# Linear attention and a feed-forward layer in one kernel: projection on half the array's rows, VectorE in written order, an early x chunk

## The chip, the cores and the metric

The kernel runs on one core of a Trainium2 chip. The metric is the device time of that core in microseconds (us). The engines are TensorE (PE in the profile, with its weight loads as PEld), VectorE (DVE), ScalarE (ACT), GpSimd (POOL), and SyncE (SP), whose queue issues nearly all DMAs.

## The reference, cut to what matters

```python
batch, n_heads, seq, head_dim = (8, 8, 576, 64);  d_feat = 128     # q, k, v, w_phi
n_tokens, d_model, d_ff = (4608, 512, 2048)                        # w_in, w_out, alpha

def phi(x):
    proj = np.einsum('bhsd,df->bhsf', x, w_phi)
    proj = proj - np.max(np.abs(proj), axis=-1, keepdims=True)
    return np.concatenate([np.exp(proj), np.exp(-proj)], axis=-1)
q_p, k_p = (phi(q), phi(k))
kv = np.einsum('bhsf,bhsd->bhfd', k_p, v)
z = np.sum(k_p, axis=2)
num = np.einsum('bhsf,bhfd->bhsd', q_p, kv)
den = np.einsum('bhsf,bhf->bhs', q_p, z)[..., None] + 1e-06
attn = num / den

x = attn.transpose(0, 2, 1, 3).reshape(B * S, H * D)
h = x @ w_in
g = np.maximum(h, 0.0) + alpha * np.minimum(h, 0.0)
out = g @ w_out
```

All data are float32; the weights of the feed-forward layer come as float64 and are decoded on the chip.

## The kernel before, in words

**Attention.** The 64 (batch, head) products go two heads at a time: 32 pairs. A pair's k and q lie transposed in one tile `raw`, head 0 on partitions 0 to 63 and head 1 on 64 to 127, in nine tiles of 128 columns (tile 4 holds the last 64 keys and the last 64 queries). `project` (line 202) multiplies each tile with `w_sb`, a block-diagonal 128 x 256 matrix that holds `w_phi` twice: one matmul over all 128 array rows gives both heads' projections. It does so in five chunks (`CHUNKS`) of 2, 2, 1, 2 and 2 tiles into `pj`, two PSUM buffers. Of each chunk VectorE takes the absolute maximum `m` (L221) and writes `t = pj - m` to SBUF (L222); then the buffer is free. For keys ScalarE makes `exp(t)` and `exp(-t)` (`k_exp`, tiles `xk` and `k4`). `k_acc` (L255) forms kv on TensorE, each head on its own 64 array columns. `k_sum` (L245 to L247) adds the key tiles on VectorE in three steps (`y`, `z`, `z`), and `k_z` (L265) sums the rest over partitions by a matmul with ones. `kv_turn` (L276) transposes; `q_exp` (L286, L292) transposes the query part of `t`, and ScalarE takes exponentials; `num` (L302) and `den` (L316) are the two products, the latter on 32 array columns each. The denominator then goes through a small DMA into 9 columns (`d9`), is inverted on VectorE (L332, L333), written to `rec_d` in device memory and read back over all partitions as `rr`; GpSimd multiplies (L343), and SP stores the result to `x_d`.

**Feed-forward layer.** All products are made of three passes with a high and a low part, so a matrix product of one 128 x 128 block takes three matmuls of 512 columns. Its 2048 hidden columns are split: pass 1 does the first five blocks of 128 (`NF1`), pass 2 the other eleven. Tokens go in nine chunks of 512 (`C2`). Pass 1 of chunks 0 to 6 runs between the attention's work: `fetch` (L388) reads the chunk from `x_d` as `xr`, `split` makes `xh` on VectorE (L95) and `xl` on GpSimd (L98), `up` gives `h` (L372 to L374), `act_g` (L161 to L168) forms `g`, `gh` and `gl` on ScalarE and VectorE, and `down` gives `o` (L378 to L380), stored to `part_d`. Behind the attention come the first step of pass 2 with chunk 0 (`load_x(0)`: four reads of 256 KB, L497, and the casts to `x2hl`), pass 1 of chunks 7 and 8, and then the rest of pass 2. `decode` (L129) makes float32 weights of float64 ones: a scale on ScalarE (L138), four integer steps on VectorE (L139 to L142), the rest on GpSimd and ScalarE; ten blocks (`NA`) are written to `w_d` and read back later by POOL's queue (L463).

**Order.** Every unit of work stands in a list `todo` with a time in units of one pair: pair i's unit comes at i plus its entry in `AT`, and chunk c of pass 1 between its start and that of the next chunk, which `F0`, `FR` and `FB` give. The list is sorted, and in that order TensorE and SP get their instructions (`manual_schedule`, L456). A planner with its own model of durations sets the order on VectorE, ScalarE and GpSimd; it held to the written order where `keep_in_program_order` stands. Each engine then works through its list strictly in order.

## Time and profile before

| what | value |
|---|---|
| median of 3 runs | 1289.01 us (1287.61 to 1291.89) |
| the profiled execution | 1286.31 us, its span 1284.5 us |
| mean granted TensorE clock | 0.978 |
| PE busy | 1201.5 us (94%) |
| DVE busy | 661.7 us (52%) |
| ACT busy | 553.7 us (43%) |
| POOL busy | 205.1 us (16%) |

The first 135 us are attention and decoding alone (pairs 0 to 8), up to about 657 us attention and pass 1 alternate, and the rest is the feed-forward layer alone. In the rows of groups, a name such as `pj<-w_sb,raw` is output and inputs, `128*128 128x256` the array part and the output, and the part behind the bar the busy time, the mean time of one, and the idle time ahead of them with what ended it. A float32 matmul leaves two records (576 for the 288 projections), a matmul of the feed-forward layer and a transpose one. In a timeline, records of one kind in a row are merged into one line with their count, and the second column is the time from the first one's start to the last one's end.

### The profile page before, as it was taken

What the parts mean: (1) busy time and instruction counts of PE and PEld (TensorE: products, weight loads), DVE (VectorE), ACT (ScalarE), POOL (GpSimd) and SP (SyncE); (2) the same over time, 40 slices, a digit from 0 to 9 for tenths busy, and PEclk for the clock granted to TensorE, in tenths of its full rate; (3) what the DMA queues carried; (4) which work ended last, traced back from release to release, by engine and by line L of the source; (5) the groups of instructions that cost most, each with busy time, mean ns of one, the idle gap of its engine ahead of it and who ended that gap; (6) DMA issues with size and microseconds to landing.
All of it is one profiled execution on the core that took longest, in us unless ns stands there. A gap on an engine that the chain in (4) does not pass through costs nothing.

```text
span 1284.5 us, 16532 instructions
## 1 busy us (share of the span) xinstructions
PE 1201.5 (94%) x6272; PEld 909.1 (71%) x6272; DVE 661.7 (52%) x1134; ACT 553.7 (43%) x1113; POOL 205.1 (16%) x209
## 2 busy tenths in 40 slices
PE   6888699989999899998959999999999999999998
PEld 4555467667766577665647888888888888888886
DVE  6678766656665665667715275333333242324232
ACT  4556455535555454454623364333333233333332
POOL 2223412121130301315404043000000000000000
PEclk9999899999999899999979999999999999999999
DMA  4244425243433524435254141211202020202010
GB/s 160 82 128 140 131 91 159 91 158 100 159 99 117 175 77 147 128 111 180 80 199 148 41 140 58 75 57 42 98 1 99 1 99 1 98 1 99 1 66 33
DMA packets 67806, 124.18 MB, mean 97 GB/s; under 512 B 14224, under 2 KB 19472, under 8 KB 67088
## 3 DMA queue, kind: packets, MB, share of 16 engines
q1 hardware_dynamic: 67008, 117.90, 28.3%
q0 software_dynamic: 720, 5.24, 1.1%
q8 instruction: 49, 0.80, 0.3%
q14 instruction: 29, 0.24, 0.1%
HBM read 89.27 MB, written 33.70 MB: 96 GB/s over the span
## 4 chain that ended last, share of the span: by engine, by line
PE 67%; DVE 13%; DMA 12%; ACT 3%; issue 3%; POOL 2%; SPq 1%; DVEq 0%; ACTq 0%; POOLq 0%
PE h L372 9%; PE h L374 9%; PE h L373 9%; PE po L378 7%; PE po L379 7%; PE po L380 7%; PE pj L213 5%; PE kv L255 3%; DMA xr<-x_d 3%; DMA rr<-rec_d 2%; DVE t L222 2%; DMA raww<-w_out_dram 2%; DVE m L221 2%; DMA raww<-w_in_dram 2%; DMA rec_d<-r 2%
## 5 line engine op out<-in xcount | busy, mean ns | idle before, releaser
L163 DVE SCALAR_TENSOR_TENSOR g<-r,aln,g 128x512 f32<-128x512 f32 x144 | 112.4, 781 | 289.3 <-ACT g L162 287.5
L161 ACT ACTIVATE r<-h 128x512 f32<-128x512 f32 x144 | 86.0, 597 | 271.4 <-PE h L374 271.3
L213 PE MATMUL pj<-w_sb,raw 128*128 128x256 f32 x576 | 158.8, 400 | 43.8 <-DVE t L222 37.1
L213 PEld LDWEIGHTS pj<-w_sb,raw 128*128 128x128 f32 x576 | 109.1, 196 | 74.8 <-issue 46.2
L378 PE MATMUL po<-gh,w 128*128 128x512 f32 x396 | 155.2, 392 | 0.0
L379 PE MATMUL po<-gh,w 128*128 128x512 f32 x396 | 155.1, 392 | 0.0
L380 PE MATMUL po<-gl,w 128*128 128x512 f32 x396 | 153.2, 392 | 0.0
L98 DVE TENSOR_TENSOR gl<-g,gh 128x512 fp32r<-128x512 f32 x144 | 105.4, 732 | 74.1 <-ACT gh L94 73.5
L94 ACT CAST gh<-g 128x512 fp32r<-128x512 f32 x144 | 89.6, 622 | 101.5 <-DVE g L163 101.1
L221 DVE TENSOR_REDUCE m<-pj 128x4 f32<-128x512 f32 (+1 forms) x160 | 100.3, 628 | 23.1 <-PE pj L213 22.4
L222 DVE TENSOR_TENSOR t<-pj,m 128x512 f32<-128x512 f32 (+1 forms) x160 | 100.8, 631 | 2.1
L372 PE MATMUL h<-xh,w 128*128 128x512 f32 x180 | 88.1, 489 | 13.2 <-DVE xh L95 13.2
L372 PE MATMUL h<-x2hl,w 128*128 128x512 f32 x220 | 87.0, 396 | 13.9 <-ACT x2hl L94 13.9
L343 POOL TENSOR_TENSOR s<-s,rr 128x576 f32<-128x576 f32 x31 | 44.5, 1434 | 281.7 <-DMA rr<-rec_d 272.1
L378 PE MATMUL o<-gh,w 128*128 128x512 f32 x180 | 85.4, 475 | 2.6 <-ACT gh L94 1.6
L373 PE MATMUL h<-x2hl,w 128*128 128x512 f32 x220 | 86.6, 394 | 0.0
L374 PE MATMUL h<-x2hl,w 128*128 128x512 f32 x220 | 86.6, 394 | 0.0
L380 PEld LDWEIGHTS po<-gl,w 128*128 128x128 f32 x396 | 74.3, 188 | 16.7
L379 PEld LDWEIGHTS po<-gh,w 128*128 128x128 f32 x396 | 74.3, 188 | 16.7
L378 PEld LDWEIGHTS po<-gh,w 128*128 128x128 f32 x396 | 74.3, 188 | 16.7
L162 ACT ACTIVATE g<-h 128x512 f32<-128x512 f32 x144 | 85.6, 595 | 0.0
L294 ACT ACTIVATE qf<-qt 128x512 f32<-128x512 f32 x128 | 68.8, 599 | 30.5 <-PE qt L292 30.3
(77 smaller groups left out, 2084.6 us busy)
## 6 DMA issues: line engine op xcount, KB each, us to landing
raw<-kq_dram SPq DMA_DIRECT2D x32, 576.0 KB
xr<-x_d SPq DMA_DIRECT2D x17, 1024.0 KB
v<-v_dram SPq DMA_DIRECT2D x32, 320.0 KB
rr<-rec_d SPq DMA_DIRECT2D x64, 144.0 KB
x_d<-s SPq DMA_DIRECT2D x32, 288.0 KB
part_d<-os SPq DMA_DIRECT2D x36, 256.0 KB
pt<-part_d SPq DMA_DIRECT2D x9, 1024.0 KB
raww<-w_in_dram SPq DMA_DIRECT2D x32, 256.0 KB
```

The lines of the kernel that those rows point to most:

```text
L94: return act.copy(dst, src)
L98: return eng.tensor_tensor(dst, src, f(hi), op=ALU.subtract)
L163: dve.scalar_tensor_tensor(g, r, aln[:, ff : ff + 1], g, op0=ALU.mult, op1=ALU.add)
L213: pe.matmul(ps[:, j].rearrange("p h f -> p (h f)"), lhsT=c["raw"][:, tp * P : (tp + 1) * P], rhs=w_sb, start=True, stop=True,)
L221: dve.tensor_reduce(m, ps, axis=AX.X, op=ALU.max, apply_absolute_value=True)
L222: dve.tensor_tensor(c["t", ch][:, :, j0 : j0 + w].rearrange("p h j f -> p j h f"), ps, m.unsqueeze(3).broadcast_to([P, w, 2, FD]), op=ALU. ...
L372: pe.matmul(ps, lhsT=wt[0][:, ws], rhs=xh, start=n == 0, stop=False)
L373: pe.matmul(ps, lhsT=wt[1][:, ws], rhs=xh, start=False, stop=False)
L374: pe.matmul(ps, lhsT=wt[0][:, ws], rhs=xl, start=False, stop=n == NK - 1)
L378: pe.matmul(ps, lhsT=wt[2][:, ws], rhs=gh, start=first, stop=False)
L379: pe.matmul(ps, lhsT=wt[3][:, ws], rhs=gh, start=False, stop=False)
L380: pe.matmul(ps, lhsT=wt[2][:, ws], rhs=gl, start=False, stop=last)
```

## The change

It has five parts.

1. **Projection.** `w_sb` is now `w_phi` once on partitions 0 to 63 and once on 64 to 127. Each head has its own matmul with 64 array rows and 128 output columns, into a `pj` buffer of its own, so one chunk takes both buffers. There are three chunks of 4, 3 and 2 tiles instead of five.
2. **z.** For the first nine pairs (`ZP`) `k_sum` does nothing, and `k_z` has ten matmuls (five key tiles, two heads) instead of two.
3. **VectorE's order** is now the written one too. So that each VectorE step can have a time of its own, `decode`, `act_g`, `split`, `k_sum` and the denominator's steps are cut into units with offsets (`WE`, `WO`, `FG`, `FX`, `FS`, `ks`, `d9`, `rr`, `xs`), and the times in `AT` are new.
4. **Chunk 0 of pass 2** is read and cast inside `todo` (`first_x`, at `X0T`), by one read of 1024 KB, and no more behind the attention.
5. Pass 1's chunks start 0.2 to 0.3 pairs later (`F0`, `FB`), the fetch of a chunk stands 0.6 instead of 0.5 pairs ahead of it. The last pair's multiply with `rr` goes from VectorE to GpSimd.

```diff
-CHUNKS = ((0, 1), (2, 3), (4,), (5, 6), (7, 8))
+CHUNKS = ((0, 1, 2, 3), (4, 5, 6), (7, 8))
+ZP = 9
 AT = dict(
     ld=-0.95,
-    p=(0.0, 0.10, 0.36, 0.46, 0.60),
-    ke=(0.30, 0.48),
-    ks=0.50,
-    ka=0.90,
-    kz=1.150,
-    kt=1.153,
-    kr=1.52,
-    q=(1.66, 1.74, 1.80),
-    d=2.149,
-    n=2.152,
-    dv=2.50,
-    x=2.85,
+    p=(0.0, 0.44, 0.70),
+    ke=(0.20, 0.56),
+    ks=(0.50, 0.60, 0.82),
+    ka=0.71,
+    kz=1.004,
+    kt=1.08,
+    kr=1.40,
+    q=(1.46, 1.52, 1.58),
+    n=2.006,
+    d=2.008,
+    d9=2.44,
+    dv=2.68,
+    rr=2.88,
+    x=3.12,
+    xs=3.26,
 )
-F0 = 9.0
+F0 = 9.2
 FR = 3.3
-FB = 6.8
-FL = 0.5
-FX = 0.25
+FB = 7.1
+FL = 0.60
+FX = (0.44, 0.36, 0.28, 0.20)
+FG = (0.10, 0.20)
+FS = 0.14
+WE = 0.14
+X0T = (31.2, 32.35, 32.45, 33.3, 33.4)
+WO = 0.40
...
         def project(ch):
             tps = CHUNKS[ch]
             w = len(tps)
...
-            ps = ps_pj.tile([P, w, 2, FD], F32, tag="pj", name=f"pj{i}_{ch}")
+            if ch < 2:
+                c["t", ch] = wk.tile([P, 2, 4 + ch, FD], F32, tag=f"t{ch}", name=f"t{i}_{ch}", bufs=P_BUFS)
+            t, j0 = (c["t", 1], 3) if ch == 2 else (c["t", ch], 0)
+            ps = [ps_pj.tile([P, w, FD], F32, tag="pj", name=f"pj{i}_{ch}_{h}") for h in range(2)]
             for j, tp in enumerate(tps):
-                pe.matmul(
-                    ps[:, j].rearrange("p h f -> p (h f)"),
-                    lhsT=c["raw"][:, tp * P : (tp + 1) * P],
-                    rhs=w_sb,
-                    start=True,
-                    stop=True,
+                for h in range(2):
+                    hs = slice(h * D, (h + 1) * D)
+                    pe.matmul(
+                        ps[h][:, j, :],
+                        lhsT=c["raw"][hs, tp * P : (tp + 1) * P],
+                        rhs=w_sb[hs],
+                        start=True,
+                        stop=True,
+                    )
+            for h in range(2):
+                m = wk.tile([P, w], F32, tag="m", name=f"m{i}_{ch}_{h}", bufs=4)
+                dve.tensor_reduce(m, ps[h], axis=AX.X, op=ALU.max, apply_absolute_value=True)
+                dve.tensor_tensor(
+                    t[:, h, j0 : j0 + w], ps[h], m.unsqueeze(2).broadcast_to([P, w, FD]), op=ALU.subtract
                 )
...
         def k_z():
-            for h in range(2):
-                pe.matmul(
-                    c["kv"][h * D : (h + 1) * D, 1], lhsT=ones, rhs=c["z"][:, :, h, :], start=False, stop=True
-                )
+            if i < ZP:
+                zs = [c["x", 0][:, :, :, j, :] for j in range(4)] + [c["x", 1][:, :, :, 0, :]]
+            else:
+                zs = [c["z"]]
+            for j, z in enumerate(zs):
+                for h in range(2):
+                    pe.matmul(
+                        c["kv"][h * D : (h + 1) * D, 1],
+                        lhsT=ones,
+                        rhs=z[:, :, h, :],
+                        start=False,
+                        stop=j == len(zs) - 1,
+                    )
...
+    def first_x():
+        st = {}
+
+        def fetch0():
+            st["xr"] = xhl.tile([P, NK, C2], F32, tag="xr", name="xr2_0", bufs=XR_BUFS)
+            nc.sync.dma_start(st["xr"], x_d[:, :, :C2].rearrange("k p s -> p k s"))
+            xs[0] = []
+
+        def cast0(j):
+            if j % 2 == 0:
+                st["xq"] = qp.tile([P, 2, 2, S], F32R, tag="qf", name=f"x2hl0{j}", bufs=QH_BUFS)
+            xh, xl = (st["xq"][:, n, j % 2, :C2] for n in range(2))
+            rnd(act, xh, st["xr"][:, j])
+            low(dve, xl, st["xr"][:, j], xh)
+            xs[0].append((xh, xl))
+
+        return [fetch0] + [lambda j=j: cast0(j) for j in range(NK)]
...
-    with tc.manual_schedule(engines={mybir.EngineType.PE, mybir.EngineType.SP}):
+    with tc.manual_schedule(engines={mybir.EngineType.PE, mybir.EngineType.SP, mybir.EngineType.DVE}):
         for _, u in todo:
             u()
```

What this does to the order is shown at three places. The first is TensorE around the end of a pair's first chunk, in the stretch where pass 1 runs beside the attention; `pj` is the projection, `d`, `kv<-z`, `n` are denominator, z and numerator of earlier pairs, `h` and `o` pass 1's products. Before:

```order
L213 MATMUL pj_0_2361<-w_sb,raw_2179 128x256 x2
L378 MATMUL o_1_0_2356<-gh_1_1_2138,w_89 128x512
L379 MATMUL o_1_0_2356<-gh_1_1_2138,w_89 128x512
L380 MATMUL o_1_0_2356<-gl_1_1_2139,w_89 128x512
L213 MATMUL pj_1_2386<-w_sb,raw_2179 128x256 x2
L378 MATMUL o_1_0_2356<-gh_1_2_2230,w_90 128x512
L379 MATMUL o_1_0_2356<-gh_1_2_2230,w_90 128x512
L380 MATMUL o_1_0_2356<-gl_1_2_2231,w_90 128x512
L316 MATMUL d_2395<-qf_2305,sf_2281 32x288 x8
L265 MATMUL kv_2345<-z_2270,ones 64x256 x2
L302 MATMUL n_0_2411<-qf_2305,sf_2281 64x288 x4
L302 MATMUL n_1_2417<-qf_2305,sf_2281 64x288 x4
```

The same place in the changed kernel; the two projection rows, one for each head, are the last of four such couples in a row:

```order
L247 MATMUL pj_0_0_2540<-w_sb,raw_2376 128x128
L247 MATMUL pj_0_1_2541<-w_sb,raw_2376 128x128
L309 MATMUL kv_2500<-z_2477,ones 64x256 x2
L350 MATMUL n_0_2568<-qf_2441,sf_2414 64x288 x4
L350 MATMUL n_1_2574<-qf_2441,sf_2414 64x288 x4
L364 MATMUL d_2580<-qf_2441,sf_2414 32x288 x8
L428 MATMUL h_1_4_2519<-xh_1_2169,w_92 128x512
L429 MATMUL h_1_4_2519<-xh_1_2169,w_92 128x512
L430 MATMUL h_1_4_2519<-xl_1_2170,w_92 128x512
```

The projection now stands in one piece directly ahead of z, numerator and denominator. The second chunk stands between the transposes `kt` and `qt_0` in the same way, and the third directly ahead of `k_acc`.

The second place is VectorE where a chunk of pass 1 begins (chunk 3; `xh` are its casts, `d_16` and `r_16` the inversion for pair 16, `aw` and `ew` the decoding). Before:

```order
L332 TENSOR_SCALAR d_16_3184<-d_16_3184 128x9
L333 RECIPROCAL r_16_3242<-d_16_3184 128x9
L221 TENSOR_REDUCE m_4_3269<-pj_4_3266 128x4
L222 TENSOR_TENSOR t_3_3229<-pj_4_3266,m_4_3269 128x2x2x128
L95 CAST xh_3_3272<-xr_3_3221 128x512 x4
L139 TENSOR_SCALAR aw_0_0_3341<-aw_0_0_3341 128x256
L140 SCALAR_TENSOR_TENSOR aw_0_0_3341<-raww_0_0_3254,aw_0_0_3341 128x256
```

In the changed kernel:

```order
L279 TENSOR_TENSOR y_3489<-xk_3441 128x1024
L283 TENSOR_TENSOR z_3512<-y_3489 128x512
L104 CAST xh_3_3519<-xr_3_3491 128x512
L382 TENSOR_SCALAR d_16_3461<-d_16_3461 128x9
L383 RECIPROCAL r_16_3523<-d_16_3461 128x9
L256 TENSOR_REDUCE m_2_0_3537<-pj_2_0_3531 128x2
L257 TENSOR_TENSOR t_1_3463<-pj_2_0_3531,m_2_0_3537 128x256
L256 TENSOR_REDUCE m_2_1_3540<-pj_2_1_3532 128x2
L257 TENSOR_TENSOR t_1_3463<-pj_2_1_3532,m_2_1_3540 128x256
L104 CAST xh_3_3519<-xr_3_3491 128x512
L286 TENSOR_TENSOR z_3512<-z_3512,k_0_121 128x512
L104 CAST xh_3_3519<-xr_3_3491 128x512 x2
```

The first cast, which waits for the chunk's DMA, now stands ahead of the inversion, of the emptying of the third chunk's two buffers and of the last step of z.

The third place is SP behind the attention. Before, from the last pair's store on:

```order
L344 DMA x_d<-s_5884 128x576
L419 DMA part_d<-os_6_2_5947 128x512
L419 DMA part_d<-os_6_3_5966 128x512
L497 DMA xr_5992<-x_d 128x512
L497 DMA xr_5997<-x_d 128x512
L497 DMA xr_6001<-x_d 128x512
L497 DMA xr_6006<-x_d 128x512
L388 DMA xr_7_6054<-x_d 128x4x512
```

In the changed kernel, from the read of chunk 0 on, which stands ahead of the store of pair 28:

```order
L515 DMA xr_0_6013<-x_d 128x4x512
L397 DMA x_d<-s_5792 128x576
L377 DMA d_29_6036<-ds_6000 128x1x9
L384 DMA rec_d<-r_29_6091 128x9
L389 DMA rr_6129<-rec_d 64x576 x2
```

Behind the last pair's store there now stand one `part_d` store and then at once the read of chunk 7 (`xr_7`).

More of the change, by code (lines that the diff above doesn't have):

```diff
@@ L353, in attention_units @@
             (AT["q"][1], lambda: q_exp(1)),
-            (AT["ks"], k_sum),
+            *((AT["ks"][n], lambda n=n: k_sum(n)) for n in range(3)),
             (AT["kr"], kv_turn),
@@ L388, in fetch, with split @@
             nc.sync.dma_start(xr[0], x_d[:, :, cs].rearrange("k p s -> p k s"))
-        def split():
-            xh = xhl.tile([P, NK, C2], F32R, tag="xh", name=f"xh1_{c}", bufs=1)
-            xl = xhl.tile([P, NK, C2], F32R, tag="xl", name=f"xl1_{c}", bufs=1)
-            for n in range(NK - 1, -1, -1):
-                ins = rnd(dve, xh[:, n], xr[0][:, n])
-                if c < B - 2:
-                    tc.keep_in_program_order(ins)
-                last[0] = low(pool, xl[:, n], xr[0][:, n], xh[:, n])
-            gs.append([(xh[:, j], xl[:, j]) for j in range(NK)])
-        cur = {}
+        xt = []
+        def split(n):
+            if not xt:
+                xt.append(xhl.tile([P, NK, C2], F32R, tag="xh", name=f"xh1_{c}", bufs=1))
+                xt.append(xhl.tile([P, NK, C2], F32R, tag="xl", name=f"xl1_{c}", bufs=1))
+            xh, xl = xt
+            j = NK - 1 - n
+            rnd(dve, xh[:, j], xr[0][:, j])
+            last[0] = low(pool, xl[:, j], xr[0][:, j], xh[:, j])
+            if n == NK - 1:
+                gs.append([(xh[:, j], xl[:, j]) for j in range(NK)])
+        cur, ga = {}, {}
         def up(ff, n):
@@ L560, in fused_kernel @@
     for c in range(B - 1, NC2):
-        loads, units = ffn1_units(c)
+        fetch, splits, steps = ffn1_units(c)
+        units = [u for us in steps for _, u in us]
         if c == B - 1:
-            for u in loads:
+            for u in [fetch] + splits:
                 u()
@@ L568, in fused_kernel @@
         else:
-            tail += loads + units
+            tail += [fetch] + splits + units
     merge(tail, decode_units(range(NA, NA + ND)))
```

189 lines of the change are left out of this document (106 added, 83 removed).

## The prediction

> **What bounds the kernel now.** I read the page first, then a table of busy time by stage, then TensorE's waits, then its timeline at single places. The page's row for TensorE:
>
> ```profile
> PE 1201.5 (94%) x6272; PEld 909.1 (71%) x6272; DVE 661.7 (52%) x1134; ACT 553.7 (43%) x1113; POOL 205.1 (16%) x209
> ```
>
> By stage (length, then busy us of PE, PEld, DVE, ACT, POOL with their counts, granted clock, DMA share, GB/s):
>
> ```profile
> 0.00:160.00 160.00, 125.49 (x797) 83.45 (x797) 115.72 (x225) 80.22 (x173) 48.45 (x58) 0.93 0.40 129
> 160.00:320.00 160.00, 153.02 (x923) 109.87 (x921) 98.61 (x177) 82.12 (x173) 32.80 (x30) 0.98 0.38 120
> 320.00:480.00 160.00, 153.58 (x941) 108.11 (x941) 103.91 (x178) 83.38 (x176) 32.41 (x31) 0.98 0.39 124
> 480.00:640.00 160.00, 147.22 (x912) 103.57 (x907) 110.37 (x198) 82.61 (x179) 49.48 (x46) 0.99 0.42 131
> 640.00:676.00 36.00, 22.13 (x109) 16.40 (x108) 7.50 (x13) 8.93 (x20) 4.41 (x5) 0.81 0.55 179
> ```
>
> From 160 to 640 us TensorE idles 26 us of 480, so time taken off it there comes off the span. Before 160 it idles 34 us with VectorE at 72%: there a chain of both sets the pace. Around 656 us it stands still. Its largest waits in the whole run (total, times, longest):
>
> ```profile
> PE pj L213 <- DVE t L222: 37.1, 23, 5.1
> PE h L372 <- ACT x2hl L94: 13.9, 1, 13.9
> ```
>
> So TensorE bounds the attention stages, and what it waits for is VectorE emptying the projection's buffers, and chunk data at two places.
>
> **A. The projection beside pass 1 (23 pairs, 9 to 31).** What one burst of two tiles costs today (start, length, operation):
>
> ```profile
> 248.66 0.50 PE L378 MATMUL o<-gh,w 128*128 128x512 f32 x1
> 248.99 0.39 PE L379 MATMUL o<-gh,w 128*128 128x512 f32 x1
> 249.22 0.39 PE L380 MATMUL o<-gl,w 128*128 128x512 f32 x1
> 249.45 1.03 PE L213 MATMUL pj<-w_sb,raw 128*128 128x256 f32 x4
> 250.12 0.58 PE L378 MATMUL o<-gh,w 128*128 128x512 f32 x1
> 250.54 0.40 PE L379 MATMUL o<-gh,w 128*128 128x512 f32 x1
> ```
>
> A 512-column matmul takes 0.23 us (249.22 - 248.99). From 249.22 to 250.54 are 1.32 us; less two such matmuls, the burst takes 0.86, a tile 0.43, a pair's nine tiles 3.87 us. The new matmuls have 128 columns and two records each. The transposes are the nearest row for a record of 128 columns that brings new weights each time:
>
> ```profile
> 116.52 1.04 PE L292 MATMUL qt<-ident,t 128*128 128x128 f32 x8
> 117.40 0.38 PE L286 MATMUL qt_t<-ident,t 128*128 128x128 f32 x2
> ```
>
> Eight in 0.88 us: 0.11 each. A tile now has four such records, two for each head. If the heads, on different array rows, run side by side, it takes 0.22, if one after the other, 0.44. No record here uses part of the rows, but `den` uses 32 columns each:
>
> ```profile
> L316 PEld LDWEIGHTS d<-qf,sf x8: 106/108/109, 252.7 to 252.7; 128*32 128x32 f32 x8
> ```
>
> Eight weight loads of 0.108 us start within 0.1 us, so parts of the array do load side by side when they differ in columns. I take 0.22: 1.98 us a pair. Against it stand changes between array shapes:
>
> ```profile
> 246.02 0.40 PE L374 MATMUL h<-xl,w 128*128 128x512 f32 x1
> 246.35 1.95 PE L255 MATMUL kv<-xk,v 128*64 128x256 f32 x16
> ```
>
> The way into column parts costs 0.10 (246.35 instead of 246.25), and the first matmul behind such a stretch another 0.10 (248.66 to 248.99 is 0.33, not 0.23). I take 0.2 for each additional change. There are four a pair: into each of three bursts, and out of the second to the transposes; the first and third run on into column parts that were entered from the full array before. So 1.98 + 0.8 = 2.78 instead of 3.87: 1.09 saved a pair, **25 us** in 23 pairs. Bounds: a gain of 43 (changes free, 1.89 x 23) and a loss of 20 (0.44 a tile: 3.96 + 0.8 = 4.76, 0.89 more x 23).
>
> The Trainium skill, "TensorE: Matmul & The Clock Gate", section "Measured speedup vs the span model", gives 3.07 for four row parts instead of 4. Estimated with that, a couple would take 0.22 x 4 / 3.07 = 0.29, the nine tiles 0.6 us more, and the forecast below would be 14 us higher, about 1248. No run here shows it.
>
> **B. The opening (pairs 1 to 8).** z moves from VectorE to TensorE:
>
> ```profile
> L245 DVE TENSOR_TENSOR y<-xk 128x1024 f32<-128x1024 f32 x32 | 41.2, 1287 | 45.4 <-ACT xk L238 45.4
> L246 DVE TENSOR_TENSOR z<-y 128x512 f32<-128x512 f32 x32 | 23.4, 730 | 2.0
> L247 DVE TENSOR_TENSOR z<-z,k 128x512 f32<-128x512 f32 x32 | 21.9, 684 | 2.2 <-ACT k L233 1.9
> L221 DVE TENSOR_REDUCE m<-pj 128x4 f32<-128x512 f32 x128 | 87.0, 680 | 21.8 <-PE pj L213 21.3
> L221 DVE TENSOR_REDUCE m<-pj 128x2 f32<-128x256 f32 x32 | 13.4, 418 | 1.2 <-PE pj L213 1.1
> ```
>
> VectorE loses 1.29 + 0.73 + 0.68 = 2.7 us a pair. TensorE gains eight matmuls in column parts, 16 records, as many as the `kv` row above shows in 1.95 us; without the last one's end they follow at 0.11, so 1.7 us. What a pair takes there now, from one denominator to the next:
>
> ```profile
> 61.31 1.18 PE L316 MATMUL d<-qf,sf 128*32 128x288 f32 x16
> 78.47 1.18 PE L316 MATMUL d<-qf,sf 128*32 128x288 f32 x16
> 85.53 1.10 PE L213 MATMUL pj<-w_sb,raw 128*128 128x256 f32 x4 [1.43 <-DVE t L222]
> 91.89 1.18 PE L316 MATMUL d<-qf,sf 128*32 128x288 f32 x16
> 121.94 1.18 PE L316 MATMUL d<-qf,sf 128*32 128x288 f32 x16
> ```
>
> Four pairs from 61.31 to 121.94: 15.2 us each. The one from 78.47 to 91.89 took 13.42 with 1.43 of waiting, so TensorE's work is 12.0. Changed: 12.0 - 1.09 + 1.7 = 12.6. The written order leaves one wait: the third burst needs both buffers of the second empty, four VectorE steps of 384 columns at (0.42 + 0.68) / 2 = 0.55, together 2.2 us, while only ten transposes (1.1 us) stand between. So 12.6 + 1.1 = 13.7, a gain of 1.5 x 8 = **12 us**. Bounds: 0 (something else keeps 15.2) and 21 (TensorE alone, 2.6 x 8).
>
> **C. The first chunk of pass 1.** SP, VectorE, TensorE:
>
> ```profile
> 136.45 0.58 SPq L388 DMA_DIRECT2D xr<-x_d  x1
> 143.46 3.59 DVE L95 CAST xh<-xr 128x512 fp32r<-128x512 f32 x4 [6.48 <-DMA xr<-x_d]
> 143.94 0.80 PE L372 MATMUL h<-xh,w 128*128 128x512 f32 x1 [8.42 <-DVE xh L95]
> ```
>
> The read took 7.0 us, a cast 0.9. Its new place is 0.6 pairs ahead, 0.6 x 13.7 = 8.2 us, about enough: I take **6** of the 8.4 us; bounds 0 and 9.
>
> **D. VectorE in written order, to 640 us.** A pair lasts some 20 us there. The bursts now stand 0.44, 0.26 and 0.30 pairs apart (5 to 9 us) with at most four steps of 0.68 to empty both buffers, where two bursts stood 0.10 pairs (2 us) apart; most of the waits on `t` should go, say 10 us of this stretch's 26. But at each of six chunk starts VectorE comes to the first cast 0.16 pairs (3.2 us) behind the fetch, needs 7.0 and so stands 3.8 us; behind it queue the inversion, the third burst's emptying (4 x 0.42) and z's last step. With the cast that makes 7 us where TensorE wants the buffers for the next burst after 0.30 pairs, 6 us: 1 us each, 6 in all. Net **4 us** gained; bounds a gain of 20 (three quarters of the idle time) and a loss of 30 (1.3 us at each pair).
>
> **E. Behind the attention.** TensorE, then SP and VectorE:
>
> ```profile
> 644.08 2.16 PE L302 MATMUL n<-qf,sf 128*64 128x288 f32 x16
> 656.96 0.39 PE L380 MATMUL o<-gl,w 128*128 128x512 f32 x1
> 671.21 0.79 PE L372 MATMUL h<-x2hl,w 128*128 128x512 f32 x1 [13.87 <-ACT x2hl L94]
> 675.63 0.39 PE L372 MATMUL h<-xh,w 128*128 128x512 f32 x1
> ```
>
> ```profile
> 653.31 0.58 SPq L326 DMA_DIRECT2D d<-ds  x1
> 665.75 14.89 SPq L388 DMA_DIRECT2D xr<-x_d  x2
> 673.77 3.62 DVE L95 CAST xh<-xr 128x512 fp32r<-128x512 f32 x4 [1.89 <-DMA xr<-x_d]
> ```
>
> With chunk 0 read early, pass 2's first twelve matmuls (12 x 0.23 = 2.8 us) follow at once. What is late next is chunk 7, which needs the last pair: TensorE takes it up at 675.63 today. It no longer stands behind four reads (8.0 us from 665.75 to the cast at 673.77, against 7.0 in C) and a restart at low clock (twelve matmuls in 4.4 us): 2.6 us. SP reaches the last denominator some 2 us sooner (0.43 pairs behind it instead of 653.31 - 644.08 = 9.2 us). Four steps of pass 1 (4 x 3 x 0.23 = 2.8 us) move behind the last pair, where they fill time. With the four issues themselves I take **8 us**; bounds 3 and 13. From 676 us on nothing is removed; the decoding of two blocks comes later there, under a VectorE that is busy 37% (225.57 of 608.50 us in the same table's next row).
>
> ```profile
> 676.00:1284.50 608.50, 600.09 (x2604) 487.71 (x2602) 225.57 (x347) 216.42 (x397) 37.59 (x40) 1.00 0.18 61
> ```
>
> **Sum:** 25 + 12 + 6 + 4 + 8 = 55 us off the span of 1284.5: 1229.5. The median of the runs stands 4.5 above this span, so 1234.
>
> **Rivals.** *The heads do not run side by side.* Weight loads or matmuls of the two halves queue, a tile takes 0.44, and from 0.34 on (9 x 0.34 + 0.8 = 3.87) the projection costs time. For it: no row shows a split by rows, and 128 columns of weights keep the loader as busy as the multiplier (0.11 each). Against it: the split by columns does run side by side. A is then a loss of 20, B one of 4 (12.0 + 0.89 + 1.7 + 1.1 = 15.7); with C, D and E it comes to 6 above before, 1295: slower. The Trainium skill, same page, section "LDWEIGHTS (loading the stationary operand)", says that a load's time goes with the columns and not the rows, by which half the rows would save nothing in a load; no run here shows it.
>
> *VectorE's order turns waits around.* Steps that wait for a DMA or ScalarE hold the emptying behind them. For it: in D one such place a chunk, and decoding stands in every pair. Against it: VectorE is busy 61 to 69% of this stretch. Price: D at its loss of 30 instead of a gain of 4, so 21 off, 1268.
>
> *The side parts do nothing.* The opening is paced by something else and the end by its chain of small DMAs: B and C 0, E 3; 25 + 4 + 3 = 32 off, 1257.
>
> **Chances.** Forecast 0.67 (its own range 1210 to 1255), order 0.14, side parts 0.08, no side-by-side 0.11. The range from 1208 (changes at half price, 34 in A, with 18 in B and 15 in D, and C and E as taken) to 1278 (beyond the second rival) leaves out the first rival and the far low end. About 0.3%, 4 us, is what a measurement can tell from no change: faster 0.86, same 0.03, slower 0.11.
>
> **What would show it.** A: four-tile bursts of 16 records lasting about 0.9 us, halves starting together; at 1.7 us it is wrong. B: denominators 13 to 14 us apart before 120 us. C: the wait on `xh` near pair 9 under 3 us. D: TensorE waits on `t` under 10 us in all beside pass 1, VectorE waiting on `xr` at chunk starts. E: an idle piece of 4 to 9 us ahead of chunk 7 in place of 13.9. The forecast is wrong if the halves queue, or if TensorE's idle time beside pass 1 grows.

## The result

The changed kernel takes 1239.84 us (median of 4 runs, 1239.14 to 1241.81) against 1288.31 us for the kernel before on the same chip: a ratio of 0.962 with an interval of 0.960 to 0.965. Its profiled span is 1239.8 us, 44.7 below the 1284.5 of before.

The page's row for TensorE and the table by stage, of the profile after (columns as in the prediction):

```profile
PE 1187.8 (96%) x6992; PEld 888.1 (72%) x6992; DVE 656.7 (53%) x1170; ACT 552.4 (45%) x1113; POOL 207.0 (17%) x210
```

```profile
0.00:160.00 160.00, 134.74 (x1139) 91.81 (x1139) 102.09 (x213) 79.08 (x174) 43.64 (x56) 0.95 0.40 130
160.00:320.00 160.00, 158.80 (x1178) 110.68 (x1176) 116.78 (x215) 92.28 (x194) 37.95 (x34) 1.00 0.40 128
320.00:480.00 160.00, 158.42 (x1190) 106.26 (x1188) 114.48 (x211) 91.21 (x192) 39.40 (x35) 1.00 0.47 152
480.00:600.00 120.00, 117.94 (x846) 78.77 (x843) 79.49 (x150) 66.14 (x139) 29.85 (x27) 0.99 0.44 136
600.00:640.00 40.00, 28.12 (x109) 21.99 (x107) 19.58 (x31) 11.53 (x26) 18.34 (x19) 0.87 0.56 197
```

Beside pass 1 (160 to 600 us) TensorE now stands still for 4.8 us of 440, where it stood still for 26 of 480, and the granted clock is 1.00, 1.00 and 0.99 instead of 0.98, 0.98 and 0.99. From 600 to 640 it stands still for 12 of 40 us at clock 0.87. Its largest waits (total, times, longest):

```profile
PE kt L324 <- ACT s L357: 12.2, 7, 2.6
PE pj L247 <- DVE t L257: 10.3, 20, 1.6
PE h L428 <- ACT w L103: 9.0, 1, 9.0
```

The wait on VectorE's `t` went from 37.1 to 10.3 us. Two waits are new: `kt` waits for ScalarE's copy of `s` in seven pairs, six of them in the opening (11.8 us), and chunk 7 waits 9.0 us behind the attention.

Where the 44.7 us came from can be read off the starts of the denominators' matmuls (`d`, one group a pair) in the two timelines:

| stretch | before, us | after, us | difference |
|---|---|---|---|
| start to the 1st denominators | 31.4 | 35.8 | +4.4 |
| 1st to 9th (opening, first chunk) | 137.8 | 132.5 | -5.3 |
| 9th to 29th (beside pass 1) | 416.6 | 375.0 | -41.5 |
| 29th to 32nd | 57.2 | 50.0 | -7.2 |
| 32nd to the last matmul | 635.8 | 640.6 | +4.8 |

More than all of it, 48.7 us, was gained in the 23 pairs beside pass 1. The opening with the first chunk gave 0.9 us in all, and what follows the attention became 4.8 us longer. A pair's denominators now follow its numerators, where they stood ahead of them, so the mark stands 2.1 us later in a pair (591.21 to 593.30 for the last one): 2.1 of the first row's 4.4 us are this. In the last row it is made up for by 11 matmuls of pass 1 that moved behind the last denominators (180 of `o` instead of 169, 2.5 us).

The three bursts of one pair, with what stands around them, in TensorE's timeline after (start, length, operation):

```profile
260.02 0.39 PE L436 MATMUL o<-gl,w 128*128 128x512 f32 x1
260.33 1.16 PE L247 MATMUL pj<-w_sb,raw 64*128 64x128 f32 x16
261.43 0.65 PE L309 MATMUL kv<-z,ones 128*64 128x256 f32 x4
...
268.59 0.60 PE L324 MATMUL kt<-ident,ks 128*128 128x128 f32 x4
269.12 0.94 PE L247 MATMUL pj<-w_sb,raw 64*128 64x128 f32 x12
269.99 0.66 PE L340 MATMUL qt<-ident,t 128*128 128x128 f32 x4
...
273.00 0.40 PE L436 MATMUL o<-gl,w 128*128 128x512 f32 x1
273.33 0.72 PE L247 MATMUL pj<-w_sb,raw 64*128 64x128 f32 x8
273.97 1.95 PE L294 MATMUL kv<-xk,v 128*64 128x256 f32 x16
```

The lengths of the bursts, 1.16, 0.94 and 0.72 us, differ by 0.22 for each tile: four records in the time of two. Counted from the end of what stands before (0.23 us for the `o` matmul, 0.43 for `kt`), the bursts take 1.18, 0.97 and 0.74 us. That is 2.89 a pair. The first four transposes behind take 0.41 here and 0.36 in a run below without the halves (264.28 to 264.64 there), so with the way back it is 2.94.

The other two places are in ScalarE's and TensorE's timelines of one opening pair (idle time before, and what ended it, in brackets):

```profile
98.77 2.00 ACT L270 ACTIVATE xk<-t 128x1024 f32<-128x1024 f32 x2
102.49 0.43 ACT L146 ACTIVATE aw<-raww 128x256 f32<-128x256 f32 x1 [1.72 <-DMA raww<-w_out_dram]
102.83 0.68 ACT L357 COPY s<-n 128x288 f32<-128x288 f32 x2
```

```profile
103.26 0.66 PE L324 MATMUL kt<-ident,ks 128*128 128x128 f32 x4 [1.97 <-ACT s L357]
```

`kt` needs one of the three buffers of `ps_m`, and the two parts of `n` and `d` hold all three. ScalarE frees the first one with its copy of `s`, but in its order, which the planner still makes, the scaling of a weight block stands ahead of that copy and waits for its load.

And behind the attention, on SP's queue, on POOL and on TensorE:

```profile
590.58 1.10 SPq L389 DMA_DIRECT2D rr<-rec_d  x2
600.87 0.33 SPq L397 DMA_DIRECT2D x_d<-s  x1
601.29 0.58 SPq L377 DMA_DIRECT2D d<-ds  x1
```

```profile
588.39 1.26 POOL L556 DMA_DIRECT2D w<-w_d  x2 [5.33 <-ACT qf L342]
599.41 1.43 POOL L394 TENSOR_TENSOR s<-s,rr 128x576 f32<-128x576 f32 x1 [9.77 <-DMA rr<-rec_d]
```

```profile
620.10 0.76 PE L428 MATMUL h<-xh,w 128*128 128x512 f32 x1 [9.04 <-ACT w L103]
```

The inverses of the last pair but one land 8.8 us after their issue (590.58 to 599.41), beside two reads of decoded weights. The store that needs them stands ahead of the last pair's `d` read on SP, so that this read goes out at 601.29, 8.0 us after the last denominators started (593.30); before it was 10.3 (642.97 to 653.31). From there the chain runs on to chunk 7, on SP's queue and on VectorE:

```profile
613.31 0.37 SPq L444 DMA_DIRECT2D xr<-x_d  x1
```

```profile
619.01 4.66 DVE L104 CAST xh<-xr 128x512 fp32r<-128x512 f32 x4
```

The first of these casts ends at 619.96 us, and chunk 7's first matmul starts at 620.10. ScalarE's `w`, which that matmul's row names, ends at 620.11 and is by the code no input of it.

### The profile page after: what moved, and what is told of

The parts are those of the page before. It is cut to its first block, busy times and chain, and to the rows that moved or that the text cites. A ratio compares the mean times of both kernels' runs of the same rounds, so it can differ in the third digit from the quotient of the medians.

```text
span 1239.8 us, 17895 instructions
## 1 busy us (share of the span) xinstructions
PE 1187.8 (96%) x6992; PEld 888.1 (72%) x6992; DVE 656.7 (53%) x1170; ACT 552.4 (45%) x1113; POOL 207.0 (17%) x210
## 4 chain that ended last, share of the span: by engine, by line
PE 68%; DMA 12%; DVE 9%; POOL 3%; ACT 3%; issue 3%; SPq 2%; DVEq 0%; POOLq 0%; ACTq 0%
PE h L428 9%; PE h L430 9%; PE h L429 9%; PE po L434 7%; PE po L435 7%; PE po L436 7%; PE pj L247 4%; DMA rr<-rec_d 3%; PE kv L294 3%; PE o L434 2%; PE n L350 2%; DMA raww<-w_out_dram 2%; PE o L436 2%; PE o L435 2%; DMA raww<-w_in_dram 2%
## 5 line engine op out<-in xcount | busy, mean ns | idle before, releaser
L256 DVE TENSOR_REDUCE m<-pj 128x4 f32<-128x512 f32 (+2 forms) x192 | 104.1, 542 | 108.2 <-PE pj L247 108.1
L247 PE MATMUL pj<-w_sb,raw 64*128 64x128 f32 x1152 | 105.8, 303 | 16.8 <-DVE t L257 10.3
L247 PEld LDWEIGHTS pj<-w_sb,raw 64*128 64x128 f32 x1152 | 83.8, 198 | 51.1 <-issue 44.8
L257 DVE TENSOR_TENSOR t<-pj,m 128x512 f32<-128x512 f32 (+2 forms) x192 | 107.2, 558 | 6.6
L394 POOL TENSOR_TENSOR s<-s,rr 128x576 f32<-128x576 f32 x32 | 47.4, 1480 | 273.8 <-DMA rr<-rec_d 239.1
L428 PE MATMUL h<-xh,w 128*128 128x512 f32 x180 | 78.9, 438 | 12.4 <-ACT w L103 9.0
L434 PE MATMUL o<-gh,w 128*128 128x512 f32 x180 | 78.9, 438 | 2.6 <-ACT gh L103 1.6
```

The source lines that it names most:

```text
L247: pe.matmul(ps[h][:, j, :], lhsT=c["raw"][hs, tp * P : (tp + 1) * P], rhs=w_sb[hs], start=True, stop=True,)
L256: dve.tensor_reduce(m, ps[h], axis=AX.X, op=ALU.max, apply_absolute_value=True)
L257: dve.tensor_tensor(t[:, h, j0 : j0 + w], ps[h], m.unsqueeze(2).broadcast_to([P, w, FD]), op=ALU.subtract)
L428: pe.matmul(ps, lhsT=wt[0][:, ws], rhs=xh, start=n == 0, stop=False)
L434: pe.matmul(ps, lhsT=wt[2][:, ws], rhs=gh, start=first, stop=False)
```

## The experiments

All were compared with the kernel before on their own chip. The table gives, from each run's profile, the mean distance of denominators in the opening (1st to 8th) and beside pass 1 (9th to 29th), and the time from the last denominators to chunk 7's first matmul and to the last matmul. The first column of before is from its 1st to its 7th, since its 8th stands behind the wait for the first chunk.

| run | median, us | ratio (interval) | opening, us a pair | pass 1, us a pair | to chunk 7, us | to the last matmul, us |
|---|---|---|---|---|---|---|
| before | 1288.31 | 1 | 15.1 | 20.83 | 32.7 | 635.8 |
| the change | 1239.84 | 0.962 (0.960 to 0.965) | 16.08 | 18.75 | 26.8 | 640.6 |
| full_rows | 1259.91 | 0.979 (0.975 to 0.983) | 16.43 | 19.55 | 27.3 | 638.8 |
| dve_planned | 1276.52 | 0.991 (0.988 to 0.994) | 16.85 | 20.39 | 21.2 | 635.0 |
| z_vector | 1237.99 | 0.961 (0.958 to 0.965) | 15.49 | 18.82 | 26.4 | 637.9 |
| weights_early | 1243.55 | 0.966 (0.962 to 0.970) | 13.99 | 19.91 | 27.7 | 638.8 |
| early_first | 1224.28 | 0.952 (0.950 to 0.955) | 14.21 | 18.75 | 26.9 | 638.7 |
| scale_behind | 1222.43 | 0.951 (0.948 to 0.953) | 13.63 | 18.79 | 26.6 | 638.3 |
| ef_z_vector | 1234.13 | 0.957 (0.955 to 0.960) | 15.23 | 18.78 | 26.3 | 639.9 |
| n2a1 | 1238.46 | 0.963 (0.960 to 0.966) | 16.01 | 18.81 | 22.5 | 639.5 |
| last_pair | 1237.24 | 0.961 (0.957 to 0.964) | 15.69 | 18.82 | 24.5 | 637.9 |
| late_x | 1238.17 | 0.963 (0.960 to 0.966) | 15.49 | 18.79 | 30.9 | 638.9 |
| ef_last_n1 | 1219.57 | 0.946 (0.944 to 0.949) | 14.11 | 18.75 | 19.8 | 632.4 |
| ef_tail | 1213.22 | 0.942 (0.939 to 0.945) | 14.35 | 18.84 | 20.6 | 628.2 |

The opening's column scatters by itself: n2a1, last_pair and late_x touch nothing there, their ScalarE orders the scaling steps there as the change's does, and they have 16.0, 15.7 and 15.5.

### The halves side by side: full_rows

```diff
-                        lhsT=c["raw"][hs, tp * P : (tp + 1) * P],
-                        rhs=w_sb[hs],
+                        lhsT=c["raw"][:, tp * P : (tp + 1) * P],
+                        rhs=w_sb[:, h * FD : (h + 1) * FD],
...
-    w2 = np.concatenate([w_phi, w_phi], axis=0)
+    w2 = np.zeros((P, 2 * FD), w_phi.dtype)
+    w2[:D, :FD] = w_phi
+    w2[D:, FD:] = w_phi
```

> Each head's matmul now multiplies over all 128 rows, with a weight matrix whose other half is zero; order, buffers, counts and VectorE's steps are those of the change, only the two heads can no longer run side by side. Theory (the halves run side by side and save about 1.2 us at each pair beside pass 1): a tile takes 0.43 instead of 0.22 us but the array is not reshaped, 9 x 0.21 - 0.8 = about 1.1 to 1.2 us more at each of 23 pairs and up to that at each of the 9 before: 1240 + 25 to 38, so 1265 to 1278 us. Rival (nearly all of the gain beside pass 1 comes from VectorE's written order and the larger bursts): under 10 us more, 1240 to 1250.

It took 1259.91 us, 20 more than the change: between the two, 5 us short of the first theory's range and 10 beyond the rival's. In its timeline the bursts of four and two tiles:

```profile
267.25 0.40 PE L435 MATMUL o<-gl,w 128*128 128x512 f32 x1
267.49 1.05 PE L246 MATMUL pj<-w_sb,raw 128*128 128x128 f32 x8
268.47 0.87 PE L293 MATMUL kv<-xk,v 128*64 128x256 f32 x6
...
273.41 0.40 PE L435 MATMUL o<-gl,w 128*128 128x512 f32 x1
273.64 1.95 PE L246 MATMUL pj<-w_sb,raw 128*128 128x128 f32 x16
275.52 0.65 PE L308 MATMUL kv<-z,ones 128*64 128x256 f32 x4
```

Two tiles more cost 0.90 us here (1.95 - 1.05) and 0.44 with the halves (1.16 - 0.72): the halves run fully side by side. From operation to operation these two bursts take 1.88 and 0.98 us instead of 1.18 and 0.74. Beyond 0.45 us a tile that leaves 0.08 on full rows, beyond 0.22 a tile 0.30 with the halves: some 0.2 us a burst is what the one additional change of array shape costs, as the prediction took it. The weight loads show the same (groups by line; the change first):

```profile
L247 PEld LDWEIGHTS pj<-w_sb,raw 64*128 64x128 f32 x1152 | 83.8, 198 | 51.1 <-issue 44.8 <-PE h L430 1.8 <-PE pj L247 1.2
```

```profile
L246 PEld LDWEIGHTS pj<-w_sb,raw 128*128 128x128 f32 x1152 | 147.5, 198 | 27.4 <-issue 18.7 <-PE qt L339 1.6 <-PE pj L246 1.2
```

One load lasts 198 ns with 64 rows as with 128, but 1152 of them cover 83.8 us instead of 147.5, since those of the two halves overlap. The pairs beside pass 1 came 0.80 us further apart (19.55 against 18.75), 16 us in the 20 pairs, less than the forecast 1.1 to 1.2. Part of the difference is shown: without the halves TensorE waited for `t` 0.4 us from 149 to 600 us, with them 4.2 us. And where a burst is followed by `o` instead of column parts, full rows are cheaper: in the pair from 397.17 us on the burst of four takes 1.70 us instead of 1.88, and this pair takes 18.84 us where the change's, from 396.84 us on, takes 18.00.

### VectorE's order: dve_planned

```diff
-    with tc.manual_schedule(engines={mybir.EngineType.PE, mybir.EngineType.SP, mybir.EngineType.DVE}):
+    with tc.manual_schedule(engines={mybir.EngineType.PE, mybir.EngineType.SP}):
```

> Everything as in the change, but VectorE's order inside the attention is again left to the planner. Theory (the written order is what took TensorE's waits away beside pass 1, 54.6 us in all less about 26 for the side-by-side projection): 20 to 30 us come back, 1260 to 1270 us, with TensorE busy under 154 of 160 us in each stage of 160 us. Rival (the prediction's step D: the order is worth 4 us, the rest comes from larger bursts that empty two buffers in turn): 0 to 8 us more, 1240 to 1248.

It took 1276.52 us, 37 more than the change, 6.5 beyond the first theory's range, on the far side from the rival. Beside pass 1 a pair takes 20.39 us instead of 18.75, which is 33 us in 20 pairs. Its stages and its two largest waits:

```profile
160.00:320.00 160.00, 147.64 (x1032) 102.69 (x1032) 101.20 (x191) 83.15 (x174) 36.81 (x34) 0.95 0.37 121
320.00:480.00 160.00, 154.44 (x1114) 104.08 (x1112) 109.75 (x204) 85.83 (x182) 35.79 (x32) 0.98 0.40 129
```

```profile
PE kt L324 <- ACT s L357: 23.7, 8, 3.9
PE pj L247 <- DVE t L257: 22.0, 19, 4.3
```

TensorE stands still for 18 of these 320 us (2.8 with the written order), and the granted clock falls to 0.95 and 0.98. With bursts of four, three and two tiles that need both buffers empty, VectorE's order is worth more than the split of the array. The two parts add to more than the whole gain (1.64 + 0.80 = 2.44 us a pair, where 2.08 were gained over before), so the bursts alone, without a written order, cost something; how much was not measured apart.

### What lengthens the opening: z_vector, weights_early, early_first, scale_behind, ef_z_vector

```diff
-ZP = 9
+ZP = 0
```

> z of all pairs is summed on VectorE; TensorE loses 8 matmuls in column parts at each of the first nine pairs (1.7 us), VectorE gains 2.7 us there. Theory (the opening is paced by PSUM buffers that ScalarE frees late, which kt waits for at each pair): the wait on kt stays and the pairs stay 16 to 17 us apart, total -3 to +8 us, 1237 to 1248. Rival 1 (TensorE's own added work is what made the pairs longer than before): 14.8 us a pair, about 12 us less, 1228. Rival 2 (VectorE was the pace before the change): over 17.5 us a pair, 10 us or more slower, over 1250.

1237.99 us, within 2 us of the change; 15.5 us a pair is inside the scatter of this column. The wait of `kt` fell from 11.8 to 1.7 us in the opening, against the theory's expectation that it stays, but others of like size came instead (`qt` behind `s` and `ds`, `kv` behind `k`, `pj` behind its issue). So neither TensorE's added work nor VectorE's relief set the pace.

```diff
-WL = 0.5
+WL = 0.75
```

> The loads of the expert weights to be decoded stand a quarter of a pair (about 4 us) earlier on SP's queue; nothing else moves by hand. Theory (ScalarE frees the PSUM buffers late partly because the scaling of a weight block waits for its load in front of the copies of s): the waits of kt in the opening fall from 12 us to 6 or less, and the time by 4 to 9 us, 1231 to 1236. Rival (the copies stand behind the exponentials of the next pair anyway): waits and time stay within 2 us, 1238 to 1242.

The total, 1243.55 us, speaks for neither. But the two stages parted: the opening's pairs came 14.0 us apart, with no wait of `kt` on `s` at all and the clock at 1.00 instead of 0.93, while the pairs beside pass 1 took 19.91 us. There the waits grew only from 5 to 11 us in all. The rest is the same work done more slowly: between the 9th and the 29th denominators 2782 records kept TensorE busy for 386.7 us where the change has 372.4, at a granted clock of 0.97 instead of 1.00. Why the later loads do this was not settled. So only the loads of the opening's blocks were moved:

```diff
-        todo.append((t - WL, lambda blk=blk: decode_load(*blk, WN)))
+        todo.append((t - (0.75 if blk[0] < NF1 else WL), lambda blk=blk: decode_load(*blk, WN)))
```

> Only the loads of the first twenty weight blocks (those decoded up to pair 11) stand a quarter of a pair earlier on SP's queue; the later ones stay as in the change. With all loads early the opening's pairs came 14.0 us apart instead of 16.1 and no time was spent on kt's wait, while beside pass 1 a pair took 19.8 instead of 18.9 us. Theory (the opening's loss is ScalarE waiting for weight loads; the loss beside pass 1 belongs to the later loads): the eighth denominator near 135 instead of 148 us and 18.9 us a pair beside pass 1, so 8 to 13 us less than the change, 1227 to 1232. Rival (whatever is gained before 150 us is lost again in pass 1, since another phase of the two streams meets there): pairs of 19.5 to 20 us beside pass 1 and 1238 to 1246 us.

1224.28 us, 15.6 less than the change: 14.2 us a pair in the opening, and beside pass 1 the change's 18.75. The reason was not the one expected, though. ScalarE's waits in the opening of this run:

```profile
ACT aw L146 <- DMA raww<-w_out_dram: 18.0, 9, 3.9
ACT aw L146 <- DMA raww<-w_in_dram: 11.7, 6, 3.1
```

It waits for weight loads longer than in the change (29.7 instead of 13.6 us). What differs is the place: with the loads earlier, the planner put the scaling behind the copies of `s` and `ds`. To tell place from time, the last run left the loads alone and moved that one step:

```diff
-        act.activation(f(a), raw[:, :, 1].bitcast(F32), AF.Copy, scale=2.0**-112)
+        with tc.issue_after(last[1].ins) if ff < NF1 and o == 0 and last[1] else ExitStack(): act.activation(f(a), raw[:, :, 1].bitcast(F32), AF.Copy, scale=2.0**-112)
...
-            act.copy(d, ps_d)
+            last[1] = act.copy(d, ps_d)
...
-        todo.append((t - WE, lambda blk=blk: decode_scale(*blk, WN)))
+        todo.append((t - (0.03 if blk[0] < NF1 and blk[2] == 0 else WE), lambda blk=blk: decode_scale(*blk, WN)))
```

> The loads of the weights stay as in the change; in ScalarE's order alone the scaling of each first quarter of the first twenty blocks, which stood between the exponentials xk and the two copies of s, stands behind the copies of s and ds. Theory (what lengthens the opening is that place: the copies that free the buffers for kt queue behind a step that waits for a load): kt's wait (12.2 us) falls under 3 us, the pairs of the opening come 14.0 to 15.0 us apart instead of 16.1, total 8 to 14 us less than the change, 1226 to 1232. Rival (the loads come too late wherever the step stands, and only earlier loads help): the wait moves to the next steps on ScalarE (sf, qf), the pairs stay over 15.7 us apart, 1236 to 1240.

1222.43 us, 17.4 less than the change, and 13.63 us a pair. ScalarE and TensorE in one opening pair:

```profile
90.61 0.69 ACT L357 COPY s<-n 128x288 f32<-128x288 f32 x2
...
92.79 0.45 ACT L146 ACTIVATE aw<-raww 128x256 f32<-128x256 f32 x1 [0.24 <-DMA raww<-w_out_dram]
```

```profile
90.04 1.18 PE L364 MATMUL d<-qf,sf 128*32 128x288 f32 x16
91.15 0.66 PE L324 MATMUL kt<-ident,ks 128*128 128x128 f32 x4
```

The copies follow the exponentials at once, and `kt` follows `d` without a wait. So the place of one step of 0.43 us in ScalarE's order was worth 17 us. The waits it caused were 12 us; with them gone the clock in the opening is 1.00 instead of 0.93, and the same 902 records that kept TensorE busy for 102.8 us in the change (32 to 149 us) took 95.6 (32 to 132).

With the cause gone, z could be tried again (early_first with ZP = 0):

> The first twenty weight blocks loaded early, and z of all pairs on VectorE. With ScalarE's copies in time this asks what step B's move of z is worth by itself. Theory (step B: VectorE's work and the waits on it then set the pace, since VectorE is busy 75.3 of 105 us there and would be at 90% with 2.7 us more a pair): 15 to 16 us a pair in the opening instead of 14.2, so 6 to 14 us more than with the early loads alone (1224): 1230 to 1238. Rival (TensorE's own work paces the opening, and z is 1.7 us of it): 12.5 to 13.2 us a pair, 8 to 13 us less, 1211 to 1216.

1234.13 us, 9.9 more than early_first, with 15.2 us a pair instead of 14.2, which is 7 us in the column's seven pairs: z on TensorE is worth 7 to 10 us, but only once ScalarE's copies are in time.

### Behind the attention: n2a1, last_pair, late_x, ef_last_n1, ef_tail

```diff
-N2A = 2
+N2A = 1
```

> One block of decoded weights (1 MB) instead of two is read back beside the last pair; the second is read with the other three later. Theory (the last pairs' small DMAs, which chunk 7 waits for, are slow because these reads fill the DMA engines: rr took 8.8 us there): rr of the last but one pair lands in 3 to 5 us, chunk 7's first matmul comes 3 to 5 us earlier after the last denominator than the 26.8 us of the change, total 3 to 5 us less, 1235 to 1237. Rival (chunk 7's start is set by the order on SP's queue, not by the traffic): 1238 to 1242, with chunk 7 within 1.5 us of 26.8 us behind the last denominator.

```diff
-AT = dict(
+AL = dict(
...
-        c = {}
+        c, AT = {}, dict(AL, d9=2.03, dv=2.20, rr=2.24) if i == NPAIR - 1 else AL
```

> For the last pair alone, the read of its denominators, the inversion and the read of the inverses stand right behind the denominators' matmuls (at 2.03, 2.20 and 2.24 pairs instead of 2.44, 2.68 and 2.88), so ahead of the store of the pair before on SP's queue. Theory (step E lost because SP issued this read 8 us behind the matmuls, held by that store): the read goes out 2 to 3 us behind the last denominators, chunk 7's first matmul comes 4 to 6 us sooner after them than 26.8 us, total 3 to 6 us less, 1234 to 1237. Rival (what follows is set by the SBUF that the decoding waits for and by the casts): chunk 7 starts earlier, but the same time is lost before 662 us, total within 2 us of the change.

For late_x the step that reads chunk 0 of pass 2 early is taken out and that chunk is read in the four reads of the kernel before:

```diff
-    todo += [(t, u) for t, u in zip(X0T, first_x())]
...
+    load_x(0)
```

> The first chunk of pass 2 is again read and cast behind the attention, in four reads, as before the change; all else as in the change. Prediction's step E (its early read takes four issues and a queue of reads away, together with chunk 7's start): 4 to 8 us more, 1244 to 1248. Rival (chunk 7's start is set by the last pair's chain, which is late anyway, and the early read only moves the idle time): within 2 us, 1238 to 1242.

The three stand at 1238.46, 1237.24 and 1238.17 us, with intervals that overlap the change's. n2a1 and last_pair did bring chunk 7 nearer to the last denominators, by 4.3 and 2.3 us, and late_x moved it 4.1 us away; yet the last matmul came 638 to 640 us behind them each time. The early read of chunk 0 by itself is worth nothing that can be measured. What was gained at chunk 7's start was lost behind it. Both repairs did what they were made for: with one block of weights the inverses of the last pair but one landed 5.4 us or less after their issue instead of 8.8 (n2a1), and the last pair's `d` read went out 1.7 us after its denominators started instead of 8.0 (last_pair).

The two repairs together, on early_first:

> The first twenty weight blocks loaded early (1224 us alone), the last pair's denominators read and inverted at once, and one block of weights instead of two read beside the last pair. Apart, the latter two brought chunk 7 2.3 and 4.3 us nearer to the last denominators (from 26.8 us), but the end only 2.7 and 1.1 us. Theory (what follows chunk 7's start, the work that VectorE does between its parts, sets the end): chunk 7 at 20 to 23 us, the end 638 us behind the last denominators as before, 1221 to 1225. Rival (the two add up): 6 us less at both, 1217 to 1219.

1219.57 us, 4.7 less than early_first, with the last matmul at 632.4: the two together gave 6.3 us there, more than apart, so the theory of this run fell. What remained is in VectorE's and TensorE's timelines of it:

```profile
625.60 4.15 DVE L104 CAST xh<-xr 128x512 fp32r<-128x512 f32 x4
629.67 1.76 DVE L107 TENSOR_TENSOR gl<-g,gh 128x512 fp32r<-128x512 f32 x1
...
633.79 0.69 DVE L107 TENSOR_TENSOR gl<-g,gh 128x512 fp32r<-128x512 f32 x1 [0.69 <-ACT gh L103]
```

```profile
631.48 0.73 PE L436 MATMUL o<-gl,w 128*128 128x512 f32 x2 [1.16 <-DVE gl L107]
633.81 0.52 PE L434 MATMUL o<-gh,w 128*128 128x512 f32 x1 [1.60 <-ACT gh L103]
```

The casts of chunk 8, which TensorE takes up only after chunk 7's twenty steps, stand ahead of the last activations of chunk 7, which it waits for. One order edge puts them behind:

```diff
-            low(el, gl, st["g"], st["gh"])
+            last[1] = low(el, gl, st["g"], st["gh"])
...
-            rnd(dve, xh[:, j], xr[0][:, j])
+            with tc.issue_after(last[1].ins) if c == NC2 - 1 else ExitStack():
+                rnd(dve, xh[:, j], xr[0][:, j])
```

> As the run with the early loads, the last pair's denominators at once and one block of weights; besides, VectorE's four casts of chunk 8, which stood ahead of the last three steps of chunk 7's activations (gl, g, gl), stand behind them; no other row of any engine's order is moved for it but a few decoding steps on VectorE. Theory (step E's gain was lost there: 4.2 us of casts, which TensorE needs only 14 us later, held the activations that TensorE waits for, 5 us of waits and a restart at low clock): 4 to 7 us less than without it, the end 632 to 634 us behind the last denominators. Rival (the decoding of eight quarter blocks at the same place takes VectorE, ScalarE and POOL anyway): within 2 us.

```profile
627.41 1.00 DVE L107 TENSOR_TENSOR gl<-g,gh 128x512 fp32r<-128x512 f32 x1 [0.35 <-ACT gh L103]
...
629.83 0.69 DVE L107 TENSOR_TENSOR gl<-g,gh 128x512 fp32r<-128x512 f32 x1 [0.69 <-ACT gh L103]
630.44 3.60 DVE L104 CAST xh<-xr 128x512 fp32r<-128x512 f32 x4
```

1213.22 us, 6.3 less, with the last matmul at 628.2. This is the fastest version of the study, 0.942 of before (0.939 to 0.945), and 2.1% below the change. Early loads and the step moved in scale_behind were not tried together with each other.

## Why the prediction was right in its total and where its steps were not

The forecast of 1234 us was 6 us below the measured time, and the likeliest case came true: faster, with the halves side by side. But that the total fell so near was luck: errors of 17 us (B with C), 13 us (E) and 4 us (A) met one of 24 us the other way (D), and the 4.5 us by which the median stood above the span before were not there after. By its steps:

**A, the projection: right.** A tile takes 0.22 us, as forecast. The bursts take 2.94 us a pair with the way back, against the forecast's 2.78 and the 3.87 of before: 0.93 saved, 21 us in 23 pairs instead of 25; full_rows, which measures the halves in place, gives 0.80 a pair, 18 us. The rival of queued halves is out (0.45 a tile in full_rows). Of the two sentences on the Trainium skill, "TensorE: Matmul & The Clock Gate": the estimate of 0.29 from the section "Measured speedup vs the span model" is not what this trace shows for two parts (0.22; four parts were not run). By its section "LDWEIGHTS (loading the stationary operand)" a load does not shorten with the rows, and the trace agrees: 198 ns with either. The loss that the rival drew from it did not come, because the two halves' loads overlap.

**B, the opening: wrong.** The step that failed is "The written order leaves one wait: the third burst needs both buffers of the second empty". It looked at TensorE and VectorE, whose orders are written, and not at ScalarE, whose order the planner makes anew for every change. A wait of 2 us on `kt` in six of these pairs, and a granted clock of 0.93 with them, made a pair 16.1 us where 13.7 were forecast. The sum itself was good: with ScalarE's step moved, the pairs came 13.63 us apart, and what was left of waits was 3.7 us on `t`.

**C, the first chunk: hidden.** The wait of 8.4 us on `xh` is gone, as TensorE's row shows:

```profile
149.49 0.50 PE L428 MATMUL h<-xh,w 128*128 128x512 f32 x1
```

But the same matmul stood at 143.94 before: behind a longer opening, what C gives does not show. In scale_behind it starts at 132.1 us, again without a wait: with the pairs as long as B took them, the read in its new place was early enough.

**D, VectorE's order: right in kind, far too small.** Of 4 us forecast, about 28 were there: 48.7 gained beside pass 1 less A's 21 (30 with full_rows' 18 for A). Idle time gives 21 of them (26 in 480 us before, 4.8 in 440 after; 0.055 less 0.011 for each of 480 us), the clock the other 7 (1.5% of 460). The step mis-sized two terms. "most of the waits on `t` should go, say 10 us" took 10 of 26 where some 21 went, and it did not count the lower clock that went with the waits (0.98 before, 1.00 now). The 6 us for chunk starts were not there: VectorE did stand for `xr` (6.5 us in four waits, the longest 3.4), but TensorE's waits on `t` from 149 to 600 us were 4.2 us in all, the longest 0.7. dve_planned shows that the order carries this: without it 1.64 us a pair come back. How much of it the order gave by itself, and how much only together with the larger bursts, stays open. The rival on VectorE's order had the sign wrong.

**E, behind the attention: wrong.** The idle piece ahead of chunk 7 did shrink, from 13.9 to 9.0 us, near the forecast's upper mark. And chunk 7's first matmul came 5.9 us nearer to the last denominators (26.8 instead of 32.7). But the step took what follows chunk 7 as unchanged ("From 676 us on nothing is removed"), and more was lost there than was gained, as the stretch of 64 us from this matmul on shows, before and after:

```profile
675.63:740.00 64.37, 61.27 (x263) 48.70 (x262) 24.39 (x28) 23.93 (x44) 13.15 (x13) 1.00 0.27 98
```

```profile
620.10:684.50 64.40, 57.56 (x219) 44.38 (x220) 36.87 (x52) 22.40 (x45) 24.40 (x23) 0.90 0.30 110
```

TensorE got through 219 records instead of 263, 10 us of work, with more waits and a granted clock of 0.90 instead of 1.00; right behind the wait of 9.0 us its matmuls came 0.43 us apart instead of 0.23. Three places that the step did not look at had to do with it. The last pair's `d` read was 2 us sooner on SP, as forecast, but still stood behind a store that waited for slow inverses. These shared the DMA engines with 2 MB of weights. And VectorE's order after the attention, again the planner's, put chunk 8's casts ahead of chunk 7's activations. Mended together, these three bring the last matmul from 638.7 us behind the last denominators (early_first; 640.6 in the change) to 628.2 (ef_tail), 7.6 below before, which is the size that E forecast.

The rival of side parts that do nothing came true in its parts (B, C and E together lost 4 us, where it gave them a gain of 3), but not in its sum, since D made up for it.

## What to carry to other kernels

When the order of some engines is written by hand and that of others is left to a planner, read the planned engines' order anew after every change, above all for steps that wait for a DMA ahead of a step that frees a buffer: one such step of 0.43 us cost 17 us here. Small waits on TensorE cost more than their length here: with them the granted clock fell and the same work took longer, so a forecast has to price the waits and the clock together. And a gain at the start of a stage is only a gain if the next thing in line is also on time: behind the attention two repairs moved the end by 1 to 3 us each alone, by 6.3 together, and the third by 4.2 more.

## What the runs showed of the hardware that was not expected

- Two matmuls on 64 rows each, with their weight loads, ran fully beside each other: 0.22 us for a tile of four records, 0.45 on full rows.
- The cost of waits beyond their length: in the opening TensorE's granted clock was 0.93 with 12 us of waits on `kt`, none longer than 2.6 us, and 1.00 without; 17 us were gained by removing 12.
- VectorE was slow beside POOL: in ef_last_n1 `gl` takes 1.76 us while POOL subtracts the four blocks of chunk 8 (the row below), and 0.69 right behind that.

```profile
626.56 6.00 POOL L107 TENSOR_TENSOR xl<-xr,xh 128x512 fp32r<-128x512 f32 x4
```
